# Pooled attention feeding a complex token mixer: batch 1's keys pooled by TensorE, another buffer for v's last keys, and a new order of pieces

## The chip, the cores and the metric

The kernel runs on one core of one Trainium2 chip. The metric is device time in microseconds (us) of one execution; lower is better. Before the change three runs gave 589.21, 589.93 and 592.08 us, so the median is 589.93.

## What is computed

The reference has two parts for 8 batches, 8 heads, 576 tokens and head size 64 (model width 512):

```python
k_p = k.reshape(B, H, 72, 8, D).mean(axis=3)          # 8 tokens pooled into one
v_p = v.reshape(B, H, 72, 8, D).mean(axis=3)
attn = softmax(q @ k_p^T / sqrt(D))                    # 576 x 72 per head
x = concat_heads(attn @ v_p)                           # 576 x 512 per batch
theta = x @ w_theta
y = w_tok_r @ (x * cos(theta)) + w_tok_i @ (x * sin(theta))    # mixes tokens
u = x + y
out = u + relu(u @ w_ch)
```

The weights arrive as 64-bit floats and are converted on the chip. The large products are made from high and low halves (three products each), which keeps float32 accuracy.

## The kernel before

All work is cut into named pieces. Each piece is a Python generator, and every `yield` ends one step of it. The string SCHEDULE (lines 30 to 139) names 2131 steps, and a loop at the end of the kernel runs them in that order; a letter v, g or a at the end of a name puts that step's free operation on VectorE, GpSimd (POOL) or ScalarE. So the string fixes the order on every engine and on SyncE's queue, which issues all the loads. Each engine works through its instructions in that order, and a step that waits holds back those behind it on its engine.

Names are a letter, the batch and the part:

- `k`, `v`: load pieces 0, 1 and 2 of a batch's keys or values (line 530 on). Pieces 0 and 1 hold 256 pools each, piece 2 the remaining 64; for v, piece 2 (the last keys) is stored twice, once for each half of the partitions.
- `K`, `V`: pool a piece (line 562 on). Batch 0's are pooled on TensorE, as eight matmuls with an identity that add up in PSUM (`pool_on_pe`, line 589). All later batches are pooled by adds on VectorE or GpSimd (`pool_sum`, lines 510 to 526). `K0`, `K1`, ... turn the pooled keys (`keys`, line 606), `V0`, ... scale and mask the values (`vals`, line 670).
- `Q`: load and turn q. `S`: scores and softmax of a row block of tokens. `X`: attention output x (line 871).
- `h0` to `h3`: convert w_theta. `w0.0` to `w4.0`: load and convert the token weights, real and imaginary; `W0` to `W4`: turn them on TensorE and split them into halves. `c0` to `c3`: convert w_ch.
- `T`: theta matmuls (three groups of four, line 947), sine and cosine, and the products with x. `Z`: halves of these. `M`: the token mix (line 1053, three groups of nine matmuls for one of 8 parts of a batch). `F`: the final product with w_ch (line 1081) and the output.

The order runs through an opening that loads and converts weights, does batch 0's attention and its theta, and ends with the first mix piece, `M0.0.0`. From there the pieces of neighbouring batches are interleaved. Batches 2 to 7 are handled in pairs: block 4 of the theta work holds the last 64 rows of two batches.

Buffers are shared by tags, and a tag with one buffer serves one tile at a time. The staging tile of piece 2 has the tag `kvr`, for keys and values of all batches and for one piece of batch 1's q; pieces 0 and 1 have the tag `kv`, except that batch 0's k0.1, v0.0 and v0.1 lie in parts of the still unused tile z. The low halves of x (tag `xl`, two buffers) are first written by T0.

```python
        if j < 2:
            st = staged(b, name, j, 2 * POOL * D, "kv").rearrange("p (c x) -> p c x", c=2)
        ...
        else:
            st = work([P, POOL * D], F32, "kvr", f"{name}rst{b}")
```

Of the kernel before, what the change touches and what calls it, by code (L numbers as in the profile page):

```python
# [138 lines left out]
"""

EARLY, V_ON_PE, K_ON_PE, Q_ON_PE, SUMS_ON_ACT = 2, 1, 1, 2, 2


@with_exitstack
def tile_attn_moe(
    ctx: ExitStack,
    tc: tile.TileContext,  # L150
# [1071 lines left out]
```

## Time and profile before

| | before |
|---|---|
| median of 3 runs (lowest, highest) | 589.93 us (589.21, 592.08) |
| the profiled execution | 588.76 us |
| its span, first to last instruction | 587.0 us |
| TensorE matmuls busy | 559.7 us (95%) |
| TensorE weight loads busy | 502.4 us (86%) |
| VectorE, ScalarE, GpSimd busy | 423.4, 307.5, 302.0 us |
| moved by DMA | 70.63 MB, mean 120 GB/s |
| mean granted TensorE clock | 0.984 of full speed |

The profiled execution is 588.76 us long, of which the span covers 587.0; the rest lies before the first and after the last instruction. Busy shares are shares of the span. Matmuls are pipelined and their ends are modelled, so a TensorE that is busy throughout is not at its peak. The granted clock tells how much of full speed the throttle allowed. Times within the span count from its start.

### The profile page before, as it was taken

The numbers are of one execution on the slowest core, as the hardware profiler recorded it, in microseconds if no ns is written. First come the engines' busy times: TensorE is split into PE (matmuls) and PEld (weight loads), VectorE is DVE, ScalarE is ACT, GpSimd is POOL, SyncE is SP. The second block draws the span as 40 slices with busy tenths as digits, with TensorE's granted clock in tenths as the row PEclk, the third lists the DMA queues.
The fourth block names the chain that finished last, engine by engine and source line by source line (L and its number), as shares of the span: only waits on it lengthen the run. The fifth ranks groups of instructions, "written<-read, shape, count | busy, mean of one in ns | idle before, by whom it ended". The sixth has DMA issues, their size and how long they took to land.

```text
span 587.0 us, 13259 instructions
## 1 busy us (share of the span) xinstructions
PE 559.7 (95%) x4904; PEld 502.4 (86%) x4904; DVE 423.4 (72%) x834; ACT 307.5 (52%) x628; POOL 302.0 (51%) x446
## 2 busy tenths in 40 slices
...
GB/s 276 273 261 114 121 51 79 114 129 131 80 140 133 151 130 132 120 180 127 108 131 139 152 121 119 132 182 103 94 92 145 116 80 49 55 88 9 41 26 89
DMA packets 191265, 70.63 MB, mean 120 GB/s; under 512 B 149600, under 2 KB 176224, under 8 KB 191200
## 3 DMA queue, kind: packets, MB, share of 16 engines
...
## 4 chain that ended last, share of the span: by engine, by line
PE 72%; DMA 10%; SPq 6%; DVE 5%; ACT 2%; POOL 1%; issue 1%; DVEq 0%; ACTq 0%; POOLq 0%
PE py L1053 36%; PE pt L947 14%; PE pf L1081 11%; SPq L863 2%; PE s L732 2%; DMA z<-in_v_dram 2%; SPq L1097 2%; DMA out_dram<-R 1%; DMA xt<-hall 1%; DMA wraw<-in_moe_w_tok_r_dram 1%; PE pv_av L894 1%; DMA kpst<-in_k_dram 1%; PE pv_av L885 1%; DMA qsst<-in_q_dram 1%; SPq L634 1%
## 5 line engine op out<-in xcount | busy, mean ns | idle before, releaser
L1053 PE MATMUL py<-WTh,zh 128*128 128x256 f32 (+1 forms) x576 | 87.6, 299 | 3.3 <-ACT zh L206 1.3
L1053 PE MATMUL py<-WTl,zh 128*128 128x256 f32 (+1 forms) x576 | 88.4, 298 | 0.0
L1053 PE MATMUL py<-WTh,zl 128*128 128x320 f32 (+1 forms) x576 | 86.8, 297 | 0.0
L1053 PEld LDWEIGHTS py<-WTh,zh 128*128 128x128 f32 x576 | 80.5, 190 | 7.1 <-issue 2.1
L191 POOL TENSOR_TENSOR en<-e_eps,ri 128x256 f32<-128x256 f32 (+3 forms) x74 | 44.3, 616 | 78.6 <-DVE ri L801 48.6
L1053 PEld LDWEIGHTS py<-WTh,zl 128*128 128x128 f32 x576 | 79.6, 189 | 3.0 <-issue 1.3
L1053 PEld LDWEIGHTS py<-WTl,zh 128*128 128x128 f32 x576 | 81.5, 192 | 0.7 <-issue 0.4
L191 POOL TENSOR_TENSOR zl<-z,zh 128x384 fp32r<-128x384 f32 (+1 forms) x68 | 53.4, 817 | 14.1 <-ACT zh L206 9.4
L206 ACT CAST zh<-z 128x1152 fp32r<-128x1152 f32 x22 | 25.3, 1154 | 49.1 <-PE py L1053 41.6
L947 PE MATMUL pt<-th,xh 128*128 128x512 f32 x148 | 42.4, 409 | 3.5 <-ACT xh L206 1.9
L1081 PE MATMUL pf<-uh,chh 128*128 128x256 f32 (+1 forms) x256 | 44.0, 297 | 0.0
L1081 PE MATMUL pf<-uh,chl 128*128 128x256 f32 (+1 forms) x256 | 43.6, 295 | 0.0
L1081 PE MATMUL pf<-ul,chh 128*128 128x256 f32 (+1 forms) x256 | 43.3, 295 | 0.0
L797 ACT ACTIVATE e_eps<-e_eps 128x576 f32<-128x576 f32 (+1 forms) x30 | 20.3, 678 | 43.9 <-DVE e_eps L792 43.9
L947 PE MATMUL pt<-tl,xh 128*128 128x512 f32 x148 | 40.6, 397 | 0.0
L947 PE MATMUL pt<-th,xl 128*128 128x512 f32 x148 | 40.2, 394 | 0.0
L951 ACT ACTIVATE g<-pt,c_magic 128x512 f32<-128x512 f32 x35 | 24.0, 686 | 30.5 <-PE pt L947 23.6
L1081 PEld LDWEIGHTS pf<-uh,chh 128*128 128x128 f32 x256 | 37.5, 188 | 2.5 <-issue 0.5
L1081 PEld LDWEIGHTS pf<-ul,chh 128*128 128x128 f32 x256 | 37.1, 188 | 1.1 <-issue 0.5
L1081 PEld LDWEIGHTS pf<-uh,chl 128*128 128x128 f32 x256 | 37.3, 188 | 0.7
L953 DVE SCALAR_TENSOR_TENSOR g<-g,pt 128x512 f32<-128x512 f32 x35 | 23.8, 681 | 17.2 <-ACT g L951 17.0
L947 PEld LDWEIGHTS pt<-th,xh 128*128 128x128 f32 x148 | 25.9, 192 | 9.3 <-ACT xh L206 2.5
...
## 6 DMA issues: line engine op xcount, KB each, us to landing
...
```

The costliest lines, as they stand in the source:

```text
L191: nc.gpsimd.tensor_tensor(out[:, r], a[:, r], b[:, r], op)
L206: nc.scalar.copy(out, src)
L634: queue.dma_start(st[32 * i : 32 * i + 32, S * c : S * c + S].rearrange("p (x a) -> p x a", a=32), q[b, 2 * j + c + 4 * (i // 2)].rearrang ...
L732: nc.tensor.matmul(scs[hh][o : o + 64, SP * c : SP * c + SP], qT[r, c, t0 + o : t0 + o + 64], kpT[r, c, SP * hh : SP * hh + SP], start=Tru ...
L797: nc.scalar.activation(e[:n], e[:n], AF.Exp, scale=scale)
L863: queue.dma_start(Ex[32 * j : 32 * j + 32, 0:m, i], Gx[32 * i : 32 * i + 32, 0:m, j])
L947: nc.tensor.matmul(pt, l[:, c, :], r[:, c, :], start=i == 0, stop=i == 11)
L951: nc.scalar.activation(g, pt, AF.Identity, bias=c_magic)
L953: nc.vector.scalar_tensor_tensor(g, g, MAGIC, pt, ALU.subtract, ALU.subtract)
L1053: nc.tensor.matmul(py[:, :n], l[:, kk, :], r[:, kw, t], start=i == 0, stop=i == 3 * NK - 1)
L1081: nc.tensor.matmul(pv[:, :n], l[:, kk, o], uhl[r][:, kk, t], start=i == 0, stop=i == 11)
L1097: (nc.scalar if b == B - 1 and i % 2 else nc.sync if b == B - 1 else queue).dma_start(out[b, t, ch0 : ch0 + 32].rearrange("(x t) a -> t x ...
```

## The change

Three edits. First, batch 1's keys are pooled by TensorE as well: a new function adds the eight parts of a piece in a PSUM bank of its own, one bank (tag `tp`) for each piece, and a copy on ScalarE or VectorE takes the sum to SBUF. The pieces K1.0, K1.1 and K1.2 thus have two steps instead of one. Second, batch 0's v0.2 is loaded into a buffer of the tag `xl` instead of `kvr`. Third, the order of all steps from the 31st on is new, and many steps change their engine; no step besides the three pieces' is added or taken away. The conditions in `vals` are only written in another way.

In the excerpt of the order below, the first part reaches from the 31st step to the first mix piece; the three short parts are those around the first mix piece of batches 2, 3 and 4.

```diff
-K0 K0a w0.0 w0.0 S0.0 h1 h1 S0.0 Q0.1 Q0.1 h1v h2 Q0.2 Q0.1v h1 Q0.2 Q0.2v S0.0 w1.0 S0.1 h1 Q0.4 Q0.4 S0.1 S0.0 S0.1
-h1 k1.2 Q0.3 K1.2v h3 S0.1 S0.0 Q0.4v S0.0g S0.2 Q0.3 S0.2 Q0.3v h2 v0.0 S0.2 S0.0v h1 k1.1 S0.1 S0.0 w0.1 S0.2 S0.1g
-w1.0 h2v h2 h1v S0.0v h3 S0.0 S0.1g w0.0g S0.0a h1 h3a v0.2 S0.2 S0.4 S0.3 S0.1 w0.0 S0.1a S0.1 w1.1 S0.3 S0.1v S0.3
-S0.4 h3 S0.2g w0.0 S0.2g w0.1 h3 V0.0 V0.2 w0.1v S0.4 S0.3 v0.1 h3 K1.1v w0.1 V0.1 S0.3 v1.2 w0.1 w0.0 w0.1 w3.1 S0.4
-h3 V0a w2.0 h3a W0 w1.1 V1.2g S0.3v k1.0 W0a S0.2 V0 S0.4 S0.3g S0.3 S0.2v S0.2 W0 S0.3a w1.0a w1.1a S0.2a X0.0 w1.0
-w1.1 w1.0 w2.0 X0.0a S0.4g w2.1 S0.3 X0.0v w1.1 w1.0 S0.4g X0.0a S0.3a S0.4 T0.0a W0 W0a w2.1 W0 S0.4a S0.4 S0.4v
-w2.0a w1.1 w3.0 w2.1a W1 Q1.0 h3 w2.0 w2.1 W1a w2.1 w2.0 W1 T0.0g K1.0v T0.0 w4.0 Q1.1 T0.0 T0.1a T0.0 T0.1g X0.2 w3.0
-T0.0 T0.1 w2.0 w3.0a X0.2a w3.0 Q1.0 X0.2a X0.2a v1.1 Q1.0a T0.2g w2.1 W1 W1a w3.1 T0.1 w3.1a T0.0 W1 T0.2v Q1.1 w3.0
-w3.1 Q1.1a W2 T0.2 Q1.2 w3.0 T0.1 w4.0 T0.2 X0.2g T0.0 w3.1 Q1.3 K1 T0.0 w4.0v w3.1 W2a T0.0a T0.3a V1.1v T0.2 Q1.2
-T0.0 W2 T0.3g T0.4a T0.0 v1.0 T0.1 T0.0 W3 T0.4g T0.2 T0.1 T0.2 T0.2 T0.1 w4.0 T0.1 W3a T0.1a T0.2 Q1.3 V1.0g T0.1
-T0.1 c0 T0.3 T0.3 w4.0 Q1.3a T0.2a W3 T0.3 W3 W3a T0.4 T0.1 T0.3 w4.0 W3 T0.3 T0.3 c0 T0.2 W4 T0.4 T0.2 W4a T0.2 W4
-T0.3 W4a T0.3a c0g c0 T0.4 c0 c0 T0.4 Q1.4 c0g W4 T0.3 Q1.2a T0.4 W2 K1a T0.4 K1 W2a c0a c0g T0.3 T0.4 W2 K1v T0.4
-S1.0 T0.3 T0.4 Z0.1a c1 c1 Z0.0v S1.0 c1a Q1.4 S1.0 Z0.0v u1 Q1.4a M0.0.0 c1 M0.0.0 c1 c1 Z0.1v M0.0.1 c1v c1v c2
...
-T2.4 T2.3 F1.0.0 T2.3g F1.2.0 Y3.2 T2.3v T2.4 T2.4 K4.1g F1.1.0 F1.0.0 T2.4 T2.4 F1.1.0 F1.2.1 K4 S3.1 F1.1.0 Y3.2
-F1.3.0 T2.4a T2.4 K4a K4.2g T2.4 F1.0.1 F1.2.0 T2.4 Z2.1a k5.0 E3.0 F1.3.0 Y3.2 K4 Z2.0g F1.1.0 F1.1.0 F1.3.0 K5.0g
-M2.1.0 M2.1.0 Z2.1v F1.3.0 M2.1.0 E3.0 M2.1.1 M2.1.0 Q4.0 v4.1 Z2.0g T2.4 T2.4 M2.1.1 M2.0.0 M2.1.1 T3.3v M2.1.1
...
-T3.3 M2.2.0g y3.2 F2.0.0 F2.2.0 T3.0v M2.3.1v T3.3 T3.3 F2.2.0 F2.0.0 S4.2 T3.3 T3.3a T3.3 K5.1g V5.2g F2.2.0 T3.2
-S4.2 E4.0 F2.0.0 T3.2 F2.2.0 T3.3v E4.0 T3.2 F2.0.0 T3.3v S4.2 F2.1.1 F2.2.1 T3.2 T3.2 F2.1.1 F2.2.1 K5 F2.2.1 F2.1.1
-S4.2v S4.4 F2.0.0 F2.2.0 S4.3 T3.2 F2.2.1 T3.2a S4.2g F2.1.1 S4.3 v5.1 F2.3.1 F2.3.1 F2.3.1 T3.2 T3.2g T3.2g Z3.1g
-F2.3.1 S4.2 Z3.0a F2.2.1 F2.0.1 F2.0.1 F2.0.1 F2.0.1 Q5.0 F2.2.0 S4.3 F2.1.0 F2.2.1 Z3.0g S4.3 S4.3g F2.1.0 M3.0.0
...
-T4.4 T4.4 T4.4 F3.0.0 T4.3 Y5.2 T4.3a T4.3 F3.1.0 F3.2.1 T4.3g k6.1 F3.0.0 F3.3.0 F3.3.0 T4.3v F3.0.1 F3.3.0 E5.0 T4.4
-Y5.2 T4.4 T4.4 K6.1g T4.4 F3.0.0 F3.2.0 F3.3.0 Y5.2 K6 F3.2.0 T4.4a T4.4 F3.2.0 T4.4 T4.4 Y5.2 Z4.0v K6a Z4.0v F3.2.0
-F3.0.0 K6 T5.3g E5.0 M4.0.0 F3.2.0 Z4.1a M4.0.0 M4.0.0 V6.2v M4.0.0 M4.0.1 M4.0.1 F3.0.0 M4.0.1 M4.1.0 Z4.1v Q6.0
...
+K0 h1 K0a h1 w0.0 S0.0 Q0.1 S0.0 h1a w0.0 Q0.2 Q0.1 k1.2 w0.1 h1 Q0.1v w0.0v Q0.2 Q0.3 K1.2 h1 Q0.4 S0.1 Q0.2v w0.0
+v0.1 h3 Q1.0 S0.0 S0.0 S0.2 S0.1 Q0.4 h2 S0.1 K1.2v k1.1 Q0.3 S0.0 S0.2 Q0.4v Q0.3v h1 S0.1 S0.0g S0.0g h2 h1 S0.2
+S0.1 S0.2 h2v S0.0 h2 h1v h1 S0.0v S0.2 S0.1g S0.1g S0.1 h3 S0.0 S0.3 S0.3 S0.4 S0.0a S0.1v w0.1 S0.3 h3a S0.3 S0.1
+S0.1v S0.4 v0.0 h3 w0.0 w1.0 S0.2g S0.2v w0.1v w0.0 K1.1 V0.1 S0.4 S0.4 w0.1 w1.0 h3 v0.2 h3 w0.1 V0.2 w3.0 K1.1a v1.2
+S0.3 V0.0 h3 w0.1 w1.0a V0v V0 S0.4 W0 S0.3v W0a w2.0 S0.2 V1.2g S0.2v W0 S0.2 S0.2a w1.0 S0.3g S0.4g w1.1 w1.1 S0.4g
+S0.3 S0.4 k1.0 S0.3a w1.0 S0.3 w1.1a X0.0 w1.1 w1.0 X0.0v S0.3a S0.4a w1.1 X0.0v X0.0a S0.4 W0 K1.0 w2.0 W0a h3a w2.0a
+T0.0g S0.4a W0 w2.1 h3 w1.1 w2.1 w3.1 w2.1a W1 v1.1 W1a T0.1a w3.0 w2.0 T0.0v w3.0a T0.0 w2.0 w2.1 T0.0 K1.0a T0.0 W1
+T0.0 T0.1g w2.0 X0.2 w3.0 X0.2a w2.1 X0.2a T0.1 Q1.0 K1 w3.0 Q1.1 w2.1 X0.2a w3.0 W1 T0.1 w4.0 Q1.0a W1v X0.2g T0.0
+T0.0 w3.1 Q1.1 w3.1a W1 Q1.4 T0.0 Q1.1a T0.2g V1.1v w3.1 W2 T0.2v w4.0 W2a T0.0a T0.3a T0.0 T0.1 T0.1 w3.1 T0.2 T0.0
+Q1.2 v1.0 T0.2 w4.0v w3.1 W2 T0.4g T0.0 T0.2 Q1.3 T0.1 T0.1 T0.2 T0.2 W3 T0.3g T0.1 w4.0 W3a T0.2 Q1.2 Q1.3 T0.3 W3
+T0.1a T0.1 T0.1 c0 T0.1 T0.3 T0.2 W3 W3a V1.0g Q1.3a W3 w4.0 T0.2a T0.3 T0.3 T0.4g w4.0 T0.3 c0 T0.4 T0.2 c0g T0.2
+T0.2 T0.3 W4 W4a T0.3 W4 K1a W4a T0.4 c0 c0 T0.4 c0 T0.4 W4 W2 T0.3a T0.3 K1 c0g T0.4 T0.3 T0.4 T0.4 c1 W2a W2 c0a
+T0.4 K1a T0.3 c0g T0.4 Z0.0v Q1.2a S1.0 Z0.1a c1 Q1.4 S1.0 c1a M0.0.0 Z0.0v c1 c1 c1 S1.0 M0.0.0 M0.0.1 Q1.4a c1v c2
...
+T2.4v T2.3a T2.3 T2.3g Y3.2 F1.2.0 T2.4 T2.4 F1.0.1 T2.4 T2.3v S3.1 Q4.0 T2.4 F1.1.0 T2.4 Y3.2 F1.1.0 F1.1.0 K4.1g
+T2.4 F1.0.0 K4 F1.3.0 F1.2.1 T2.4 Y3.2 k5.0 F1.1.0 T2.4a K4.2g T2.4 T2.4 F1.3.0 T2.4 K5.0g Z2.1v K4a F1.3.0 T3.3a K4
+M2.1.0 E3.0 Z2.1v F1.3.0 M2.1.0 M2.1.0 M2.1.1 Z2.0a M2.1.1 M2.1.1 E3.0 T3.3v M2.1.0 T2.4 Z2.0v M2.1.1 F1.1.0 F1.2.0
...
+T3.3 T3.3 T3.0v T3.0v F2.0.0 T3.3 v5.2 K5.1g S4.3 S4.2 T3.2v F2.0.0 F2.2.0 F2.2.0 F2.2.0 T3.3 T3.3 F2.2.0 T3.2 E4.0
+M2.3.1a T3.3 T3.3a T3.2 E4.0 T3.3 S4.2 F2.2.0 S4.2 T3.2 T3.3g M2.3.1g F2.2.1 T3.3v F2.1.1 T3.2 S4.2 F2.1.1 F2.2.1
+F2.2.1 T3.2 T3.2 F2.1.1 S4.2g F2.0.0 K5 F2.2.1 F2.3.1 F2.2.0 T3.2a S4.2g F2.1.1 F2.0.1 S4.3 T3.2 F2.3.1 F2.3.1 S4.2
+T3.2g v5.1 F2.0.1 F2.0.1 F2.3.1 F2.0.0 T3.2g Z3.0a F2.0.1 F2.2.1 S4.4 F2.2.1 S4.3 M3.0.0 F2.1.0 Q5.0 u4 K5a Z3.0g
...
+T4.4g F3.1.0 F3.0.0 T4.3 F3.1.0 T4.4v k6.1 Y5.2 T4.3 T4.4 T4.3a F3.0.1 F3.1.0 S5.1 T4.3 T4.3g T4.3v T4.4 T4.4 F3.3.0
+T4.4 F3.3.0 Y5.2 T4.4 E5.0 F3.0.0 F3.3.0 F3.3.0 T4.4 F3.0.0 T4.4 T4.4a T4.4 T4.4 F3.0.0 K6.1g T4.4 F3.2.0 v6.0 Y5.2
+Z4.0v V6.0g F3.2.0 K6 V6.2g K6a F3.2.0 E5.0 K6 Z4.1a V6g M4.0.0 F3.2.0 Z4.0v M4.1.0 M4.0.0 M4.0.0 T4.4 F3.2.0 M4.1.0
...
-EARLY, V_ON_PE, K_ON_PE, Q_ON_PE, SUMS_ON_ACT = 2, 1, 1, 2, 2
+EARLY, V_ON_PE, K_ON_PE, Q_ON_PE, SUMS_ON_ACT = 2, 1, 2, 2, 2
 
 
 @with_exitstack
@@ -546,7 +546,10 @@
                         )[j, hh],
                     )
         else:
-            st = work([P, POOL * D], F32, "kvr", f"{name}rst{b}")
+            if name == "vp" and b == 0:
+                st = work([P, POOL * D], F32, "xl", f"{name}rst{b}", bufs=2)
+            else:
+                st = work([P, POOL * D], F32, "kvr", f"{name}rst{b}")
             if name == "kp":
                 st = st[0:64]
                 nc.sync.dma_start(st, pools[512:])
@@ -561,6 +564,9 @@
 
     def pool(b, name, j, pe):
         st = stages[name, b, j]
+        if pe and b:
+            yield from pool_apart(b, name, j, st)
+            return
         if pe:
             pool_on_pe(b, name, j, st)
             yield
@@ -601,6 +607,33 @@
                 n = st.shape[0]
                 nc.tensor.matmul(rem, ident[0:n, 0:n], st[:, D * r : D * r + D], **steps[r])
 
+    def pool_apart(b, name, j, st):
+        if (name, b) not in pooled:
+            pooled[name, b] = [work([P, NC, D], F32, name, f"{name}{b}", bufs=2 if name == "vp" else 1), None]
+            if name == "kp":
+                pooled["kq", b] = pooled[name, b]
+        n = st.shape[0]
+        bk = bank([P, 512], "tp" if name == "kp" else "th", f"{name}p{b}_{j}")
+        pv = bk[:n, 0 : D if j == 2 else 2 * D]
+        if j < 2:
+            pv = pv.rearrange("p (c d) -> p c d", d=D)
+        for r in range(POOL):
+            nc.tensor.matmul(
+                pv, ident[0:n, 0:n], st[..., D * r : D * r + D], start=r == 0, stop=r == POOL - 1
+            )
+        yield
+        e = pick("av")
+        if j == 2:
+            dst = pooled[name, b][1] = work([n, D], F32, name + "r", f"{name}r{b}")
+            copy(e, dst, pv)
+        elif name == "kp":
+            copy(e, pooled[name, b][0][:, 2 * j : 2 * j + 2, :], pv)
+        elif e == "a":
+            nc.scalar.mul(pooled[name, b][0][:, 2 * j : 2 * j + 2, :], pv, 1.0 / POOL)
+        else:
+            nc.vector.tensor_scalar(pooled[name, b][0][:, 2 * j : 2 * j + 2, :], pv, 1.0 / POOL, None, ALU.mult)
+        yield
+
     Vrs, qTs, parts, er32 = {}, {}, {}, {}
 
     def keys(b):
@@ -669,7 +702,7 @@
 
     def vals(b):
         vm, vr = pooled["vp", b]
-        if b < V_ON_PE:
+        if b == 0:
             Vs[b] = work([P, NC, D], F32, "vp", f"vp{b}", bufs=2)
             nc.scalar.mul(Vs[b], vm, 1.0 / POOL)
             yield
@@ -678,7 +711,7 @@
         Vr = Vrs[b] = work([P, 2, D], F32, "Vr", f"Vr{b}", bufs=2)
         for y in range(2):
             r = slice(64 * y, 64 * y + 64)
-            (nc.vector if b < V_ON_PE else ENG[pick("vg")]).tensor_tensor(
+            (nc.vector if b == 0 else ENG[pick("vg")]).tensor_tensor(
                 Vr[r],
                 vr[r].unsqueeze(1).broadcast_to([64, 2, D]),
                 mask[r, y].unsqueeze(2).broadcast_to([64, 2, D]),
```

## Rows read from the trace of the kernel before

**Rows 1.** Page, part 1: each engine's busy us (share of the span) and instructions.

```profile
PE 559.7 (95%) x4904; PEld 502.4 (86%) x4904; DVE 423.4 (72%) x834; ACT 307.5 (52%) x628; POOL 302.0 (51%) x446
```

**Rows 2.** Stretches: from:to, length; busy PE, PEld, DVE, ACT, POOL; granted clock; DMA share; GB/s.

```profile
0.00:28.00 28.00, 22.70 (x160) 18.58 (x161) 20.56 (x49) 15.85 (x68) 8.00 (x18) 1.00 1.02 278
28.00:40.00 12.00, 8.92 (x57) 8.10 (x56) 9.10 (x21) 7.86 (x40) 3.97 (x7) 0.86 0.83 209
40.00:50.00 10.00, 8.21 (x83) 6.21 (x81) 7.87 (x15) 8.85 (x17) 3.50 (x5) 0.96 0.65 222
50.00:76.00 26.00, 26.00 (x177) 21.15 (x176) 24.00 (x41) 22.39 (x39) 10.91 (x15) 0.95 0.46 109
76.00:82.40 6.40, 3.21 (x46) 2.27 (x44) 6.19 (x14) 5.50 (x13) 2.86 (x4) 0.81 0.25 86
82.40:200.00 117.60, 117.60 (x1202) 105.91 (x1203) 97.14 (x193) 77.22 (x192) 64.67 (x96) 0.98 0.57 115
200.00:400.00 200.00, 191.77 (x1703) 171.13 (x1702) 147.10 (x282) 106.64 (x169) 125.98 (x183) 0.99 0.62 136
400.00:560.00 160.00, 159.91 (x1326) 147.93 (x1326) 100.19 (x200) 63.16 (x95) 79.65 (x117) 1.00 0.37 78
560.00:587.00 27.00, 21.33 (x166) 21.12 (x164) 11.21 (x26) 0.00 (x0) 2.52 (x4) 0.97 0.40 62
```

**Rows 3.** Chain of waits, 0 to 90 us: start us, us, what.

```profile
26.41 8.98 DMA z<-in_v_dram
...
35.53 3.65 PE vpp L599 x16
...
50.43 3.93 PE pt L947 x12
...
69.49 3.56 DMA qst<-in_q_dram
...
82.38 7.75 PE py L1053 x41
```

**Rows 4.** SyncE's issues, 0 to 90 us: start us, us, queue, line, out<-in.

```profile
25.05 2.15 SPq L542 DMA_DIRECT2D z<-in_v_dram  x2
...
33.04 1.41 SPq L555 DMA_DIRECT2D vprst<-in_v_dram  x2
...
47.60 0.52 SPq L441 DMA_DIRECT2D wraw<-in_moe_w_tok_r_dram  x1
...
54.88 1.99 SPq L542 DMA_DIRECT2D vpst<-in_v_dram  x2
```

**Rows 5.** What SyncE waited for, 0 to 90 us: us in total, times, longest.

```profile
SPq L555 <- DMA vprst<-in_v_dram: 3.1, 1, 3.1
...
SPq L555 <- PE vpp L602: 2.6, 1, 2.6
```

**Rows 6.** TensorE pools two pieces of batch 0's keys (timeline).

```profile
6.03 2.05 PE L599 MATMUL kpp<-kpst,ident 128*128 128x128 f32 x16
...
12.72 1.14 PE L602 MATMUL kpp<-kprst,ident 64*64 64x64 f32 x16
```

**Rows 7.** VectorE's adds for batch 1's keys (timeline).

```profile
20.69 0.73 DVE L521 TENSOR_TENSOR kprst<-kprst 64x256 f32<-64x256 f32 x2
...
32.26 1.14 DVE L521 TENSOR_TENSOR kpst<-kpst 128x512 f32<-128x512 f32 x2
...
52.87 1.66 DVE L521 TENSOR_TENSOR kpst<-kpst 128x512 f32<-128x512 f32 x2
...
54.56 0.29 DVE L526 TENSOR_TENSOR kp<-kpst 128x128 f32<-128x128 f32 x1
```

**Rows 8.** TensorE at the first mix piece of batches 2 and 4 (timeline).

```profile
226.04 1.71 PE L1053 MATMUL py<-WTh,zh 128*128 128x256 f32 x9 [1.30 <-ACT zh L206]
...
355.51 0.63 PE L1081 MATMUL pf<-ul,chh 128*128 128x256 f32 x4
...
360.43 1.33 PE L1053 MATMUL py<-WTh,zh 128*128 128x256 f32 x9 [0.40 <-DVE zh L208]
```

168 lines of the change are left out of this document (84 added, 84 removed).

## The prediction

> **What bounds the kernel now.** I read the page's first part, then the table of stretches, then the chain of waits of the opening, then SyncE's list of issues with what it waited for, then single instructions for prices. TensorE is busy 559.7 of 587.0 us [rows 1], so the time is its work plus its idle time, 27.3 us. The table says where that idle lies [rows 2]: 5.3 us in 0 to 28, 3.1 in 28 to 40, 1.8 in 40 to 50, none in 50 to 76, 3.2 in 76 to 82.4, none from 82.4 to 200, 8.2 from 200 to 400, almost none to 560, and 5.7 in the last stretch, which ends with output. The opening, up to the first token-mix matmul at 82.4 us, thus holds 13.4 us, half of it all, and after it batches 0 and 1 run without a gap. So the question has two halves: when does the first M0 piece start, and what happens to the gaps between 200 and 400 us?
>
> The chain of the opening [rows 3] ends its DMA part with the last piece of batch 0's v to arrive: v0.1 holds the chain for 8.98 us to 35.4 us. TensorE pools it in 3.65 us, and 15 us after the landing, at 50.43, the first theta matmul starts. From there TensorE is full until 76 us. A DMA wait of 3.56 us to 73.05 (the row names q's staging tile; what goes on after it is w_ch's conversion) and VectorE work follow, and M0 starts at 82.4.
>
> Why does v0.1 land so late? SyncE issues it at 25.05 (ready by 27.2), and then issues nothing until 33.04 [rows 4]. The issue at 33.04 is v1.2, which needs the one buffer that v0.2 sits in; it waited 3.1 us for v0.2's bytes and 2.6 us for TensorE to pool them [rows 5]. All loads share that queue, so the transfer rate falls from 278 GB/s in 0 to 28 to 209 in 28 to 40 [rows 2]. In 12 us at 69 GB/s less, 0.83 MB were not moved, or 3.0 us at the earlier rate.
>
> **The change, part by part.** The sum is made against the profiled execution, 588.76 us (span 587.0); the median of the runs is 589.93, 1.17 us above, and I carry that difference over.
>
> (a) **v0.2 in another buffer.** v1.2 no longer waits for v0.2, so the stop from 27.2 to 33.04 goes, unless another takes its place. v0.2 itself waited for k1.2 to be pooled; that goes too. By the tiles' sizes, 8.8 MB were asked for up to the end of v0 before; in the new order it is 8.5 MB, v0.2 being last. At 278 GB/s that is 30.6 us; before, the same division gives 31.7 against 35.4 measured, so 3.7 us behind. The last of v0 therefore lands between 30.6 and 34.3; I take 31.5, nearer the early end, as no stop now stands ahead of it. Gain: 3.9 us, ends 1.1 and 4.8. What is late next is v1.1's load: its buffer is that of k1.0, so it stands behind K1.0's pooling, and behind it on SyncE now stand Q1.1, w4.0, Q1.4, Q1.2, v1.0, Q1.3 and c0. Before, w4.0 was issued at 47.6 and v1.1 at 54.88 [rows 4]. In the new order both come right after K1.0's matmuls, at some 45 to 48 us, so w4.0 is about where it was and v1.1 some 7 us earlier. I cost this at nothing: W4 is turned only after three of the five theta pieces, and these fill TensorE's stretch from 50 us on [rows 2]. If w4.0 came 5 us later than that cover allows, M0 would be 5 us later.
>
> (b) **Batch 1's k on TensorE.** Batch 0's pieces show the price: 2.05 us for a 256-pool piece, 1.14 us for the rest [rows 6]. Batch 1 has two of the first and one of the second: 5.24 us more TensorE work. K1.2 (1.14) stands where TensorE idles 5.3 of 28 us, K1.1 (2.05) now stands just before v0's pooling, where it idled 3.1 of 12 us; both cost nothing there, and 3.19 us if their data came later than v0's. K1.0 (2.05) stands between X0.0 and T0.0, with 1.8 us idle in 40 to 50. I take half of it as hidden: +1.0, ends 0 and 2.05. The ScalarE or VectorE copies that follow stand in 28 to 50 us beside 5.3 idle us of ScalarE, and nothing but their bank waits for them.
>
> The Trainium skill's page "Trainium Kernel Development and Optimization" (Best Practices) says that matmul busy share is the wrong gauge of room on TensorE and that the share of weight loads is a good one. In 50 to 76 the matmul row is 26.00 of 26 and the weight-load row 21.15 [rows 2]. By the page another 4.8 us would fit there, so K1.0 would be free even if it slid past T0.0, and the sum below would be 1.0 us lower.
>
> (c) **VectorE is freed** of the same pooling: 0.73 for K1.2's first adds, 1.14 + 0.29 for K1.1, 1.66 + 0.29 for K1.0 [rows 7], together 4.1 us. Six other pieces ahead of M0 move on to VectorE and four off it, at 0.2 to 0.7 us each; I set this at nothing net, within 1.5 us. VectorE was busy 24.0 of 26 us in 50 to 76 and 6.2 of 6.4 in 76 to 82.4 [rows 2], so without its relief it, not TensorE, would keep M0 where it was. With K1.0's 1.95 us out of 52 to 55 and the weight rows handled a few us sooner in 28 to 50, where it idled 5.0 of 22 us, it can follow. I add no gain for it.
>
> (d) **The half-clock stretch.** TensorE stood idle before v0.1, and then its 16 matmuls took 3.65 us, against 2.05 for the same 16 of batch 0's k [rows 3, 6]; the granted clock of 28 to 40 is 0.86 [rows 2], so part of it ran at 1.2 instead of 2.4 GHz. With K1.1 and the other pieces of v in that hole the idle time shrinks; I take half of the 1.6 us back: -0.8, ends -1.6 and 0.
>
> (e) **The new order after M0.** Every batch has the same pieces between its milestones, shifted by about eight places, and some 150 change engine. From 82.4 to 200 and from 400 to 560 TensorE had no idle time to give back. From 200 to 400 it had 8.2 us. Nothing in the trace shows the new waits, so I bound them: all gaps gone, -8; doubled, +8. I take 0, since the places at the batch changes that I compared (below) are slightly worse and the copies moved off POOL slightly better.
>
> **Sum:** -3.9 + 1.0 - 0.8 = -3.7 us; 588.76 becomes 585.1, in terms of the runs 586.2. M0 should start near 78.7 us.
>
> **Rivals.** (1) *The opening does not move.* TensorE's full stretch begins when W1 has been converted and turned, as both orders put W1 ahead of T0.0; w1.1 is now asked for after 10.5 MB instead of 8.3, at 278 GB/s 38 us instead of 30. If that conversion, or K1.0's full 2.05 us, sets T0.0, the gain of (a) is lost: with T0.0 at 50.4 again, M0 is at 82.4 and the time 590. For it: TensorE already idled 1.8 us in 40 to 50, after v0 was pooled, so more than v0 was missing there. Against: VectorE and ScalarE, which convert W1, idled 5 us each in 28 to 50, and w0.1 now comes first.
>
> (2) *Slower: thinner cover at the batch changes.* Between the last theta matmul of a pair and its first mix matmul stand F pieces of the batch before, up to 0.63 us each [rows 8]; the work they hide is ScalarE's and VectorE's sine chain. The new order has 6 at M2 where there were 7, 12 for 14 at M3, 7 for 8 at M4. Today M2 waits 1.30 us and then takes 1.71 us for its first nine matmuls; M4 waits 0.40 and takes 1.33 [rows 8]. If each of the three loses two pieces' worth (1.3 us) and falls into a half-clock stretch that costs as much as the opening's (1.6), that is 3 x 2.9 = 8.7 us, less the opening's 3.7: 595. It decides from 3.7 us on, somewhat over one such loss. For it: M2's row shows wait and slow start together. Against: M4 waited 0.40 without a slow start, and one piece fewer is 0.63, not 1.3.
>
> (3) *Much better.* The wait in 76 to 82.4, where the granted clock is 0.81 [rows 2], shrinks as well, or half of the 8.2 us goes: 586.2 less 4 to 5, 582. Against: the order of W4, c0 and T0.4 ahead of M0 is almost unchanged.
>
> **How the numbers follow.** Forecast 586.2: 0.45. Rival 1: 0.25. Rival 2: 0.15. Rival 3: 0.15. A measurement of this kernel can tell about 0.5% (2.95 us) from no change, so faster means below 587.0, slower above 592.9. The forecast's own case reaches from 583.5 (a, b and d at their best: -6.4) to 590.9 (at their worst: +1.0), with 0.6 of it below 587.0: 0.27; rival 3 gives 0.15, the early side of rival 1 0.05: faster 0.47. Rival 2 puts 0.11 above 592.9, rival 1 with some of (e)'s loss 0.05: slower 0.16. The rest, 0.37, is the same. Range: from 580 (beyond rival 3's time) to 593; outside are rival 2's upper part and the far end of rival 3, under 2 in 10 together.
>
> **What would show it.** Right: SyncE without the stop at 27 to 33; a rate near 278 GB/s to about 40 us; the last of v0 landed by 33; T0.0's first matmul near 47; M0 near 78.7. Each failing names its step. If M0 comes near there and the time does not fall, (e) is wrong, and the table of 200 to 400 shows it; if T0.0 stays at 50 with v0 early, rival 1. The forecast is wrong if SyncE finds another stop of several us before 40 us, for instance at k1.0 or v1.1.

## The result, and the profile after

The changed kernel takes 583.39 us (median of 4 runs, 581.3 to 584.59) where the kernel before takes 590.42 in the same set (4 runs, 589.21 to 592.08): ratio 0.9897, 95% interval 0.9865 to 0.9929. A later set of both gave 583.46 (12 runs) against 588.0 (32 runs), ratio 0.992, 0.9887 to 0.9952. By the medians it is 4.5 to 7.0 us faster; the forecast was 3.7. Medians are over all runs, while the ratios leave out the few slow ones (two of run 2's ten below, one of the 32), which lie over 1.5% above their kernel's fastest. The size is about right. The place is not: the opening, where the forecast put its gain, did not move.

The profile's first part answers [rows 1]: TensorE is busy 0.9 us less, with 48 more matmuls, and idle 5.4 us less (580.7 - 558.8 = 21.9, before 27.3). ScalarE and POOL are relieved, VectorE is not.

```profile
PE 558.8 (96%) x4952; PEld 502.3 (87%) x4952; DVE 423.4 (73%) x834; ACT 297.6 (51%) x617; POOL 295.8 (51%) x445
```

The same stretches as [rows 2], with the same columns:

```profile
0.00:28.00 28.00, 23.44 (x169) 19.19 (x171) 20.62 (x48) 16.19 (x68) 6.02 (x17) 1.00 1.03 259
28.00:40.00 12.00, 9.70 (x82) 9.46 (x81) 7.01 (x16) 8.23 (x41) 1.05 (x2) 0.86 1.04 268
40.00:50.00 10.00, 8.52 (x87) 6.49 (x87) 7.84 (x16) 6.66 (x15) 4.62 (x8) 1.00 0.47 179
50.00:76.00 26.00, 26.00 (x191) 21.34 (x189) 23.90 (x41) 23.31 (x40) 11.90 (x16) 1.00 0.55 120
76.00:82.40 6.40, 3.80 (x46) 2.72 (x45) 6.18 (x13) 5.87 (x14) 2.84 (x4) 0.76 0.27 83
82.40:200.00 117.60, 117.60 (x1208) 105.77 (x1208) 95.15 (x193) 78.53 (x197) 65.67 (x100) 0.98 0.56 117
200.00:400.00 200.00, 195.05 (x1735) 174.30 (x1733) 150.95 (x287) 104.05 (x162) 126.49 (x191) 1.00 0.64 140
```

Two things are to be seen. In 28 to 40 us the transfer rate is 268 GB/s where it was 209, as forecast, and TensorE works 0.8 us more. Yet M0 starts at 82.11 us, where it started at 82.38. And from 200 to 400 us TensorE idles 4.95 us where it idled 8.2, at full granted clock.

Why did the faster loads not help? First SyncE's issues, which answer to [rows 4], with one wait that answers to [rows 5] (us in total, times, longest):

```profile
25.33 1.73 SPq L558 DMA_DIRECT2D vprst<-in_v_dram  x2
...
28.17 3.42 SPq L558 DMA_DIRECT2D vprst<-in_v_dram  x2
...
50.05 1.31 SPq L542 DMA_DIRECT2D vpst<-in_v_dram  x2
...
52.65 0.50 SPq L441 DMA_DIRECT2D wraw<-in_moe_w_tok_r_dram  x1
```

```profile
SPq L542 <- PE kpp L621: 5.7, 1, 5.7
```

The long stop from 27.2 to 33.04 is gone. Shorter ones are left: v1.2's two issues, 0.61 us each, start at 28.17 and 30.98, and in a second execution of the same kernel (run 9) SyncE waits 3.2 us, until 33.35, for VectorE to be done with a weight's buffer. And the last piece of v0 (v0.2, at 25.33) is issued no earlier than the last one was before (v0.1, at 25.05 [rows 4]).

Nor did the old stop leave the DMA engines idle. In the kernel before, with the columns of [rows 2]:

```profile
27.00:32.00 5.00, 4.45 (x38) 4.21 (x38) 4.65 (x12) 4.70 (x20) 3.03 (x4) 1.00 1.04 196
32.00:36.00 4.00, 1.48 (x13) 1.37 (x12) 3.93 (x9) 3.78 (x24) 0.00 (x0) 0.95 0.50 127
```

Through five of the stop's six us their share was 1.04, as high as before it; what they moved fell to 196 GB/s all the same. Only from 32 us on, with no load issued after v0.1 until 33.04, did the share fall. Why v0.1 needs 9 us is not shown. Then TensorE and POOL in the opening:

```profile
31.09 3.35 PE L621 MATMUL kpp<-kpst,ident 128*128 128x128 f32 x16 [2.30 <-DVE en L844]
34.23 2.30 PE L605 MATMUL vpp<-z,ident 128*128 128x128 f32 x16
36.37 1.90 PE L608 MATMUL vpp<-vprst,ident 128*128 128x64 f32 x16
38.10 2.00 PE L605 MATMUL vpp<-z,ident 128*128 128x128 f32 x16
```

```profile
40.41 1.84 POOL L191 TENSOR_TENSOR vprst<-vprst 128x256 f32<-128x256 f32 x2 [11.36 <-DMA vprst<-in_v_dram]
...
43.40 1.56 POOL L191 TENSOR_TENSOR en<-e_eps,ri 64x256 f32<-64x256 f32 x3 [0.38 <-PE per L869]
```

TensorE stands 2.30 us before K1.1 (the profile names a step of VectorE that had just ended) and then pools it at half clock (3.35 us; the same product took 2.05 in [rows 6]). V0's three products are queued behind it and end at 40.1 us; before they ended at 39.2. This wait is one execution's: in run 9, the same kernel, K1.1 starts without one and takes 1.95 us, and TensorE stands 1.98 us for v0.2 instead. POOL stands 11.36 us for v1.2, with S0.4's sums behind, which then wait 0.38 us more for TensorE. v1.2, though issued earlier, is not there earlier; its adds in the kernel before:

```profile
37.46 1.25 POOL L191 TENSOR_TENSOR vprst<-vprst 128x256 f32<-128x256 f32 x2 [7.35 <-DMA chl_st<-in_moe_w_tok_i_dram]
```

X0.0 starts at 45.28 (before 42.76) and T0.0 at 51.40 (before 50.23).

The first mix products, which answer to [rows 8], and batch 3's first theta product, which in the kernel before waited 0.80 us:

```profile
225.01 1.29 PE L1086 MATMUL py<-WTh,zh 128*128 128x256 f32 x9 [0.64 <-DVE zh L208]
...
354.98 2.31 PE L1086 MATMUL py<-WTh,zh 128*128 128x256 f32 x18 [0.33 <-DVE zh L208]
```

```profile
247.20 1.09 PE L980 MATMUL pt<-th,xh 128*128 128x512 f32 x4
```

M2 is reached 1.0 us earlier than before, M4 5.5 us earlier, and TensorE's last product ends 6.6 us earlier. In these two executions most of the gain lies behind M2.

### The profile page after: what moved, and what is told of

Its sections match the earlier page's. It is cut to its first block, busy times and chain, and to the rows that moved or that the text cites. A ratio compares the mean times of both kernels' runs of the same rounds, so it can differ in the third digit from the quotient of the medians.

```text
span 580.7 us, 13326 instructions
## 1 busy us (share of the span) xinstructions
PE 558.8 (96%) x4952; PEld 502.3 (87%) x4952; DVE 423.4 (73%) x834; ACT 297.6 (51%) x617; POOL 295.8 (51%) x445
## 4 chain that ended last, share of the span: by engine, by line
PE 83%; SPq 4%; DVE 4%; POOL 2%; DMA 2%; ACT 2%; issue 1%; DVEq 0%; POOLq 0%; ACTq 0%
PE py L1086 38%; PE pt L980 16%; PE pf L1114 14%; PE s L765 2%; SPq L896 2%; SPq L1130 1%; PE pv_av L918 1%; PE pv_av L927 1%; DMA out_dram<-R 1%; PE pv_px L918 1%; PE s_av L765 1%; PE wt L461 1%; PE kpp L621 1%; DMA qst<-in_q_dram 1%; PE ths L416 1%
## 5 line engine op out<-in xcount | busy, mean ns | idle before, releaser
L191 POOL TENSOR_TENSOR en<-e_eps,ri 128x256 f32<-128x256 f32 (+3 forms) x77 | 42.5, 574 | 67.5 <-DVE ri L834 58.1
L191 POOL TENSOR_TENSOR zl<-z,zh 128x384 fp32r<-128x384 f32 (+1 forms) x64 | 49.5, 804 | 17.8 <-ACT zh L206 11.5
L984 ACT ACTIVATE g<-pt,c_magic 128x512 f32<-128x512 f32 x35 | 24.0, 687 | 44.8 <-PE pt L980 40.1
L1092 DVE TENSOR_TENSOR xb<-py,xb 128x320 f32<-128x320 f32 x32 | 15.3, 479 | 24.0 <-PE py L1086 24.0
```

The costliest lines, as they stand in the source:

```text
L191: nc.gpsimd.tensor_tensor(out[:, r], a[:, r], b[:, r], op)
L984: nc.scalar.activation(g, pt, AF.Identity, bias=c_magic)
L1092: nc.vector.tensor_tensor(u, py[:, :n], u, ALU.add)
```

## The experiments

Theory: the new order after M0 made the gain, and the edits of the opening gave nothing. Rival: the opening's edits (earlier loads, VectorE freed) are felt later on. All kernels keep the computation whole.

The table has one profiled execution of each. M0, M2 and M4 are the starts of each batch's first mix product; up to each mark both orders have done the same products of T, M and F. Times in us.

```
kernel                          median (runs)  ratio [95%]              M0     M0-M2   M2-M4   M4-end
before                          -              -                        82.38  143.66  134.39  220.90
after                           583.39 (4)     0.9897 [0.9865, 0.9929]  82.11  142.90  129.97  219.71
1  new order alone              583.43 (4)     0.9892 [0.9845, 0.9938]  80.94  143.62  132.22  220.09
2  opening alone                586.24 (10)    0.9955 [0.9919, 0.9992]  81.08  144.43  132.47  220.07
3  new order from M2 on         583.86 (4)     0.9898 [0.9850, 0.9945]  79.39  142.88  133.01  219.87
4  after, V1.2 and K1.1 behind  586.32 (10)    0.9954 [0.9920, 0.9988]  85.16  144.36  128.68  219.43
5  one stretch new              593.88 (6)     1.0097 [1.0074, 1.0120]  80.39  143.53  141.48  219.95
6  new letters, old order       591.61 (6)     1.0083 [1.0053, 1.0113]  79.52  144.65  136.98  222.57
7  buffer alone                 589.34 (12)    1.0019 [0.9997, 1.0040]  82.37  143.33  133.71  220.07
8  K1 on TensorE alone          587.23 (12)    0.9993 [0.9973, 1.0014]  84.14  147.55  131.29  220.06
9  after, again                 583.46 (12)    0.9920 [0.9887, 0.9952]  81.39  143.63  128.54  220.54
10 opening alone, again         586.88 (12)    0.9993 [0.9962, 1.0024]  83.30  144.86  134.56  220.07
11 new order, old letters       594.47 (9)     1.0099 [1.0064, 1.0134]  81.17  149.79  133.43  219.80
12 after, V1.2 alone behind     582.48 (12)    0.9915 [0.9879, 0.9951]  81.01  143.62  129.99  220.01
```

Runs 1 to 4, 5 to 8 and 9 to 12 each had the kernel before beside them: 589.02, 588.16 and 588.0 us.

**Which half? Runs 1, 2, 3, 9, 10.** Run 1 is the kernel before up to M0.0.0, then the words of after, without the steps that its opening has already done:

```diff
 c1a Q1.4 S1.0 Z0.0v u1 Q1.4a
-M0.0.0 c1 M0.0.0 c1 c1 Z0.1v M0.0.1 c1v c1v c2 M0.0.1 M0.0.1 S1.0 S1.1
+M0.0.0 c1 c1 c1 M0.0.0 M0.0.1 c1v c2 M0.0.0 M0.0.1 Z0.1v c1v S1.0 M0.0.1
...
```

> The kernel before with its own opening (all steps up to M0.0.0's first, without the buffer and without batch 1's k on TensorE), and from there the order and the engine letters of the kernel after. Theory (the gain lies behind M0 and is the new order's own): M0.0.0 stays at 82.4 us as before, T3.1 comes near 247.5 us instead of 250.84, T4.0 near 296.8 instead of 303.14, and the time is 583.5 to 584.5 us, 6 us under the kernel before. Rival (the opening's edits reach on: earlier loads, or the 4.1 us of VectorE set free by K1): 588.5 to 590.5 us, T4.0 near 302 us.

It takes 583.43 us: the whole gain, without the buffer and without K1 on TensorE. T4.0 came at 296.18. Run 2 is the reverse, after's code and opening with before's words behind it; four steps that before has done by then come first:

```diff
 S1.0 c1a
-M0.0.0 Z0.0v c1 c1 c1 S1.0 M0.0.0 M0.0.1 Q1.4a c1v c2
+S1.0 Z0.0v u1 Q1.4a M0.0.0 c1 M0.0.0 c1 c1 Z0.1v M0.0.1 c1v c1v c2 M0.0.1
...
```

> The kernel after with its opening whole (buffer for v0.2, batch 1's k on TensorE, its order up to M0.0.0's first), and from there the order and the letters of the kernel before. Theory: M0.0.0 near 82.1 us, T4.0 near 303 us, and the time is 589.5 to 590.5 us, no more than 0.5 us from the kernel before. Rival (the opening's edits reach on): 583.5 to 586 us with T4.0 near 297 us. A third case, both are needed: this one and the order alone each give about half, 586 to 588 us.

It took 586.24 us, the number of the third case, and its interval is clear of 1. So it was run again beside after itself:

> The kernel with after's opening and before's order behind it once more, with more rounds: the first time it came out 2.8 us under the kernel before (ratio 0.9955), while the buffer alone and batch 1's k on TensorE alone changed nothing. Theory (the opening gives nothing, or little): 0 to 1.5 us under the kernel before, M0.0.0 at 80 to 83 us. Rival (the opening as a whole, with its own order, gives a part of the gain): 2 to 3.5 us under the kernel before, and M0.0.0 under 80.5 us or less half clock behind it.

> The kernel after, unchanged, as the yardstick of this set, and a second profiled execution of it. The three profiled executions of the opening of before had M0.0.0 at 79.4, 80.9 and 82.4 us, the two of after's opening at 81.1 and 82.1, so one execution's opening says little. Theory: M0.0.0 between 80.5 and 83 us again, M0.0.0 to the end of TensorE's work near 492.6 us as in the first profile (before: 498.95), and the time 5 to 7 us under the kernel before. Rival (the first profile was a lucky one behind M0, since the new order alone took 495.93 us there): 495 to 496 us for that part and 4 us under the kernel before.

Now the opening alone is 0.9993, with no change well inside the interval; after keeps its gain, and M0 to the end took 492.71 us in it, as in its first profile (492.58). What both intervals of the opening alone allow is 0.9962 to 0.9992, so a gain of 0.5 to 2.2 us is not ruled out. The traces show none: before's opening reaches T0.0 at 47.31 to 50.23 us and M0 at 79.39 to 82.38 in six executions (before, 1, 3, 5, 6, 11), after's at 50.35 to 52.54 and 81.08 to 83.30 in four (after, 2, 9, 10). M0 is 1.3 us later in the mean. Run 3 takes the new words from M2.1.0 on only:

```diff
 Z2.0g F1.1.0 F1.1.0 F1.3.0 K5.0g
-M2.1.0 M2.1.0 Z2.1v F1.3.0 M2.1.0 E3.0 M2.1.1 M2.1.0 Q4.0 v4.1 Z2.0g T2.4
+T3.3a M2.1.0 Z2.1v F1.3.0 M2.1.0 M2.1.0 M2.1.1 M2.1.1 M2.1.1 E3.0 T3.3v M2.1.0 T2.4 Z2.0v
...
```

> The kernel before with its own order up to batch 2's first mix product (M2.1.0), and the order and letters of after from there. Theory: what was gained between M2.1.0 (226.04 us in the kernel before, 1.0 us later than after) and T4.0 (303.14, 6.6 later) is made behind M2.1.0, so M2.1.0 stays at 226.0 us, T4.0 comes near 297.5 us and the time is 584 to 585.5 us. Rival (the zh copies and xh copies ahead of M2, at 200 to 226 us, are what counts): T4.0 near 300 us and 587 to 588 us. If the gain hangs on the whole order since M0: 589 to 590 us.

It takes 583.86 us, so by its runs most of the gain is made behind M2. Its one profiled execution does not place it so: M2 to M4 took 133.01 us, as with the old order, and M0 to the end 495.76. T4.0 as a mark, which these expectations use, flatters the new order: before has M3.1.1's third group of nine products ahead of T4.0, after has it behind, some 1.3 us of work. M4 has no such shift, hence the table's columns.

Averaged over the five executions with before's order behind M0 (before, 2, 7, 8, 10) and the five with after's (after, 1, 4, 9, 12), the parts are 144.8 against 143.6, 133.3 against 129.9 and 220.2 against 220.0: 4.8 us, of which 3.4 lie between M2 and M4. As a whole this gain is clear: M0 to the end takes 497.0 to 499.5 us in the five with the old order, 492.5 to 495.9 in the five with the new. Its split is less so. From M2 to M4 the two ranges overlap (131.29 in run 8, 132.22 in run 1), and the 1.2 us from M0 to M2 rest mostly on run 8: runs 3 and 5, with the old order up to M2, took 142.88 and 143.53. The stretch from 200 to 300 us shows in what form (columns as above; before and run 10, then after and run 9):

```profile
200.00:300.00 100.00, 95.62 (x810) 86.16 (x809) 72.04 (x140) 52.45 (x87) 66.30 (x96) 0.98 0.61 131
```

```profile
200.00:300.00 100.00, 94.76 (x844) 84.69 (x836) 71.69 (x136) 53.91 (x89) 64.78 (x95) 0.97 0.61 130
```

```profile
200.00:300.00 100.00, 97.08 (x858) 87.40 (x857) 75.88 (x148) 51.67 (x81) 65.17 (x101) 1.00 0.65 139
```

```profile
200.00:300.00 100.00, 96.55 (x853) 86.92 (x852) 75.59 (x146) 51.06 (x81) 63.55 (x100) 1.00 0.66 139
```

In the mean of the five, TensorE idles 4.7 us there with the old order and 3.2 with the new; in 300 to 400 us 3.1 and 2.3. The clock granted in 200 to 300 averages 0.98 and 0.996; 0.016 of 100 us, an estimate, is another 1.6 us. That is 3.9 of the 4.8; the rest lies inside time that the profile calls busy.

One gap of it can be followed back. Before batch 3's first theta product (T3.1) TensorE waits in all five executions with the old order, 1.8 us in the mean, and in none of the five with the new. (Run 5 below, with the new order from M2 on and the old one ahead of it, waits 0.57 us.) The rows, one from each of before, 2, 7, 8 and 10 (the answering row of after, 247.20, stands above, without a wait):

```profile
250.84 1.20 PE L947 MATMUL pt<-th,xh 128*128 128x512 f32 x4 [0.80 <-ACT xh L206]
```

```profile
250.31 1.20 PE L979 MATMUL pt<-th,xh 128*128 128x512 f32 x4 [2.32 <-ACT xh L205]
```

```profile
250.55 1.23 PE L950 MATMUL pt<-th,xh 128*128 128x512 f32 x4 [2.35 <-ACT xh L206]
```

```profile
254.75 1.20 PE L976 MATMUL pt<-th,xh 128*128 128x512 f32 x4 [0.58 <-ACT xh L205]
```

```profile
253.80 2.07 PE L979 MATMUL pt<-th,xh 128*128 128x512 f32 x4 [3.06 <-ACT xh L205]
```

xh is cast from x, and x is copied out of three banks. The last copies and casts on ScalarE, and what VectorE did meanwhile, in the kernel before:

```profile
249.55 0.59 ACT L206 COPY xa<-pv_s 128x512 f32<-128x512 f32 x1 [3.41 <-DVE xs L917]
250.17 0.62 ACT L206 CAST xh<-xa 128x512 fp32r<-128x512 f32 x1
```

```profile
247.39 0.43 DVE L917 STREAM_TRANSPOSE xs<-pv_px 128x256 f32<-128x256 f32 x1
247.76 0.75 DVE L521 TENSOR_TENSOR vprst<-vprst 128x256 f32<-128x256 f32 x2
248.55 0.23 DVE L526 TENSOR_TENSOR vpr<-vprst 128x64 f32<-128x64 f32 x1
248.69 0.77 DVE L917 STREAM_TRANSPOSE xs<-pv_s 128x256 f32<-128x256 f32 x2
```

The third copy stands behind Y3.0's transposes of the same banks (pv_s), and those stand behind V4.2's adds (0.75 and 0.23 us) on VectorE. The two only read pv_s, yet not at once: the copy starts 0.09 us after the transposes end. The Trainium skill's page "PSUM — Partial Sum Buffer" (PSUM bank collisions raise a hardware error) gives a reason for keeping two engines apart on one bank, reads included; the trace agrees in that these readers run one after the other here, in the order in which the program names them. The same in the kernel after:

```profile
244.51 0.59 ACT L206 COPY xa<-pv_s 128x512 f32<-128x512 f32 x1
...
245.30 0.63 ACT L206 CAST xh<-xa 128x512 fp32r<-128x512 f32 x1
```

```profile
244.19 0.42 DVE L208 COPY xa<-pv_av 128x256 f32<-128x256 f32 x1
...
245.69 0.77 DVE L950 STREAM_TRANSPOSE xs<-pv_s 128x256 f32<-128x256 f32 x2
```

The copy now stands ahead of the transposes, VectorE takes one of the three copies, and V4.2 runs on POOL. xh starts 1.9 us ahead of T3.1's product instead of 0.7 us. It is so in all ten executions: with the old order the copy waits 3.34 to 3.82 us for the transposes, with the new it starts 1.1 to 1.2 us ahead of them. That these three moves, and not others nearby, close the gap was not tried one by one.

**The opening's parts. Runs 7, 8, 4, 12.** Run 7 changes one line of the kernel before:

```diff
-            st = work([P, POOL * D], F32, "kvr", f"{name}rst{b}")
+            if name == "vp" and b == 0:
+                st = work([P, POOL * D], F32, "xl", f"{name}rst{b}", bufs=2)
+            else:
+                st = work([P, POOL * D], F32, "kvr", f"{name}rst{b}")
```

> The kernel before with one line changed: v0.2 lands in the buffer of x's low halves; order, letters and K1 as before. Prediction's step (a) taken alone: SyncE's stop at 27.2 to 33.04 us goes, v0.2 lands 3.5 to 4 us earlier, V0's pooling ends near 36 us instead of 39.2, T0.0's first product near 47 us and M0.0.0 near 79 us, and the time is 585 to 587 us. Rival (T0.0 is set by W1, K1.0 and S0's sums; the stretch to 76 us is full): V0's pooling ends earlier, X0.0 by at most 1 us, T0.0 stays between 48 and 51 us, M0.0.0 between 79.4 and 82.4 us as in the three profiled executions of this opening, and the time is within 1 us of the kernel before.

No gain (1.0019). SyncE's v1.2 moves from 33.04 to 27.93, and v0.1, issued ahead of it, arrives as late as ever; before, TensorE started this product at 35.53 [rows 3]:

```profile
26.04 1.79 SPq L542 DMA_DIRECT2D z<-in_v_dram  x2
27.93 2.35 SPq L558 DMA_DIRECT2D vprst<-in_v_dram  x2
```

```profile
36.32 3.53 PE L602 MATMUL vpp<-z,ident 128*128 128x128 f32 x16 [2.86 <-DMA z<-in_v_dram]
```

T0.0 came at 50.63, M0 at 82.37. The stop stood behind v0.1's issue and could not make v0.1 late.

Run 8 has K1 on TensorE and nothing else:

```diff
-EARLY, V_ON_PE, K_ON_PE, Q_ON_PE, SUMS_ON_ACT = 2, 1, 1, 2, 2
+EARLY, V_ON_PE, K_ON_PE, Q_ON_PE, SUMS_ON_ACT = 2, 1, 2, 2, 2
...
-h1 k1.2 Q0.3 K1.2v h3
+h1 k1.2 Q0.3 K1.2 K1.2v h3
```

> The kernel before with batch 1's k pooled by TensorE, each product at the place where VectorE's adds stood, its copy right behind it on ScalarE (K1.1, K1.0) or VectorE (K1.2); buffers and the rest of the order as before. Prediction's step (b) taken alone: 5.24 us more work on TensorE, of which 4.2 us lie in its waits and up to 1 us does not, 4.1 us less on VectorE; M0.0.0 within 1 us of before's 79.4 to 82.4 us and the time within 1 us of the kernel before. Rival (VectorE's freed 4.1 us are worth something, since the softening's sums wait for it): M0.0.0 under 79.4 us, the time 2 to 3 us under the kernel before. Other rival (TensorE waits for k1.1 as it does in after, 2.30 us with what is queued behind it): T0.0 behind 51 us and the time 1 to 2 us over the kernel before.

0.9993: 5.24 us more on TensorE and 4.1 less on VectorE cancel: the interval reaches from 1.6 us gained to 0.8 lost. The profiled execution had a late T0.0 (53.10) and M0 (84.14); the runs as a whole do not show that as a loss.

Runs 4 and 12 try to mend after's opening by two moves:

```diff
-S0.2 V1.2g S0.2v
+S0.2 S0.2v
...
-w1.1 w1.1 S0.4g S0.3
+w1.1 w1.1 S0.4g V1.2g S0.3
...
-w0.0 K1.1 V0.1
+w0.0 V0.1
...
-w3.0 K1.1a v1.2
+w3.0 v1.2
...
-V0.0 h3 w0.1 w1.0a V0v V0 S0.4
+V0.0 K1.1 h3 w0.1 w1.0a V0v V0 K1.1a S0.4
```

> The kernel after with two steps of its opening moved: V1.2's adds behind S0.4's sums on POOL, and K1.1's product and copy behind V0.0's on TensorE. Theory of why the opening did not move (POOL stood 11.36 us for v1.2 with S0.3's and S0.4's sums behind it; TensorE stood 2.30 us for K1.1 with V0's pooling behind it): V0's pooling ends near 36 us instead of 40.1, X0.0 starts near 43 us instead of 45.28, T0.0 comes 1 to 3 us earlier than 51.40 and M0.0.0 with it, 79.5 to 81 us; the time is 581 to 582.5 us. Rival (T0.0 is set by W1 or by K1.0 and the stretch to 76 us is full of work anyway): X0.0 moves, T0.0 and M0.0.0 by less than 0.5 us, the time within 1 us of after, 583 to 584 us.

A miss: M0 came at 85.16. k1.0 loads into the buffer that K1.1 reads, so its issue slid from 35.57 to 42.90 us, and TensorE, rid of K1.1, stood 3.14 us for v0.2 instead:

```profile
42.90 0.38 SPq L538 DMA_DIRECT2D kpst<-in_k_dram  x1
```

```profile
35.65 2.49 PE L607 MATMUL vpp<-vprst,ident 128*128 128x64 f32 x16 [3.14 <-DMA vprst<-in_v_dram]
```

Run 12 has only V1.2's move (the first two pairs of lines):

> The kernel after with V1.2's adds behind S0.4's sums on POOL and nothing else moved; with K1.1 moved as well, k1.0's load came 7 us later (42.90 instead of 35.57 us), since it waits for K1.1's buffer, and the opening became longer. Theory (POOL's 2 us for V1.2 stand ahead of S0.4's sums, for which X0.0 waits): X0.0 starts 1 to 2 us earlier than the 44 to 45 us of after's opening, T0.0 near 49 us, M0.0.0 near 80.5 us, 0.5 to 1.5 us under after. Rival (W1's turn and K1.0 set T0.0): T0.0 stays at 50.4 to 51.4 us and the time within 1 us of after.

X0.0 starts at 43.9 (44.55 in run 9), T0.0 at 50.28 (50.67): about the rival's case. At 582.48 against 583.46 us it is the lowest median of all, but the two intervals are almost one, so it can't be called better than after.

**Inside the order. Runs 5, 6, 11.** Run 6 keeps before's order and takes after's engines from M0 on, 137 letters; run 11 takes the order and keeps the letters:

```diff
-F1.0.1 F1.2.0 T2.4 Z2.1a k5.0 E3.0
+F1.0.1 F1.2.0 T2.4 Z2.1v k5.0 E3.0
...
```

> The order of the kernel before throughout; from M0.0.0's first on, each step runs on the engine that after names for it (137 of its letters change, among them Z2's casts from ScalarE and POOL to VectorE and T3.1's and T3.3's). Theory (the gaps of before stood behind casts on ScalarE that came late, so the letters carry most): M2.1.0 to T4.0 in 73 to 74 us instead of 77.10, 585.5 to 587 us in all. Rival (the place of the steps in each engine's queue carries it): the stretch stays at 76 to 78 us and the time at 588.5 to 590 us, or longer, since letters chosen for another order load an engine at the wrong moment.

> The kernel before, its opening kept; from M0.0.0's first step the order of after, but each step on the engine that before names for it. The counterpart of the letters alone, which cost 3.4 us. Theory (order and letters were found together; the stretch from M2.1.0 to T4.0 needs both): the stretch at 73 to 76 us instead of 71.5, and 587 to 591 us in all. Rival (the order is what counts, the letters are decoration): the stretch near 71.5 to 72.5 us and 583.5 to 585 us in all.

Each alone makes the kernel slower, by 0.8% and 1.0%; together they make it 0.8 to 1.1% faster. Neither is decoration. Where they lose was followed only so far: run 11 takes 149.79 us from M0 to M2, with its longest wait (2.16 us) just ahead of M2, and the longest of run 6's new waits is for a cast on ScalarE, at M3's first product:

```profile
287.30 1.33 PE L1052 MATMUL py<-WTh,zh 128*128 128x256 f32 x9 [2.21 <-ACT zh L205]
```

Run 5 takes after's words between M2.1.0 and T4.0 only; its first seam is run 3's.

> The kernel before, its opening and its order, but for one stretch: the 272 steps from M2.1.0's first to T4.0's first product stand in the order and with the letters of after (what is left of that stretch follows in the order of before). In the profiled executions so far this stretch took 77.10 us (before) and 77.19 (the opening alone), 71.51 (after), 71.63 (the new order alone) and 73.47 where only the steps behind M2.1.0 were new. Theory (the gain of the new order is made in this stretch): 71.5 to 73.5 us for the stretch, 584.5 to 586 us in all, 3.5 to 5 under the kernel before. Rival (the stretch shifts work into the next: what is gained by T4.0 is given back by M4.0.0): the stretch as short, but T4.0 to M4.0.0 over 60 us instead of 57.29, and 588 to 589 us in all.

593.88 us, slower than both cases, and M2 to M4 took 141.48. T4.0 came 74.66 us after M2, and M4 66.82 after T4.0, over the rival's 60, but for a reason that neither had: a wait at the second seam.

```profile
304.87 5.07 SPq L862 DMA_DIRECT2D eraw<-G  x8
310.03 2.05 SPq L1096 DMA_DIRECT2D out_dram<-R  x4
```

```profile
313.53 0.51 DVE L1091 STREAM_TRANSPOSE R<-xb 128x320 f32<-128x320 f32 x1 [14.01 <-DMA out_dram<-R]
```

```profile
314.56 2.74 PE L1052 MATMUL py<-WTh,zl 128*128 128x320 f32 x9 [9.89 <-DVE xb L1058]
```

An output's DMA had slid behind E4.2's eight issues on SyncE; VectorE stood 14.01 us for the buffer, and TensorE 9.89 us for VectorE. Without these 9.89 us M2 to M4 would be 131.6 us, an estimate, near the new order's 129.9. As a test of what the stretch is worth alone the run failed; it shows what one misplaced transpose and its output cost.

## Why the prediction was right and wrong

**(a) failed**, at the step "The last of v0 therefore lands between 30.6 and 34.3; I take 31.5". In after's opening TensorE's wait for it ended at 35.56 (run 9), 35.25 (run 2), 35.79 (run 10) and 34.92 (run 12); before it landed at 35.4, and in six executions of that opening TensorE's wait for it ended between 34.24 and 36.41. The forecast divided all bytes by a rate, as if one queue's stop delayed everything ("All loads share that queue, so the transfer rate falls"); but the DMA engines were busy through most of the stop, at a share of 1.04. And [rows 3, 4] held the answer: v0.1 was issued at 25.05, 2 us before the stop began, and its own transfer held the chain for 8.98 us. The new last piece is issued at 25.33 and takes about as long: in run 2 from 25.53 to 35.25. The rate did rise to 268 GB/s, but neither v0.2 nor v1.2 landed earlier for it. Of the loads behind, w4.0 was put "about where it was" and came at 52.65 us instead of 47.60; no cost of that shows, as TensorE stayed full to 76 us. Run 7 has the step by itself: -0.2 to +2.4 us, instead of -3.9.

**(b)** K1 on TensorE was put at +1.0 net of cover, ends 0 and 2.05; run 8, which has VectorE's relief in it too, shows -1.6 to +0.8 us. The size holds roughly. K1.1, costed at nothing, is where TensorE waited 2.30 us in the first profile, but not in run 9. Whether K1.0 was free, as the Trainium skill's page "Trainium Kernel Development and Optimization" (Best Practices) would have it by the weight-load share, or cost something that VectorE's relief gave back, that interval cannot tell.

**(c)** VectorE's freed time, counted as nothing, is in the same interval. **(d)** The half-clock stretch of the opening is not a matter of this change, so its -0.8 did not come: the granted clock of 28 to 40 us is 0.86 in both first profiles, and 1.00 in run 3 with the old opening as in run 2 with the new.

**(e) was mis-sized:** taken as 0 within 8 us, it measured -4.8 in the traces, about all of the gain. The step that failed is "the places at the batch changes that I compared ... are slightly worse": the F pieces that cover a wait were counted, not what stands ahead of the last copy and cast on ScalarE and VectorE. That this is what counted is shown at T3.1 alone. The places that the forecast compared did not decide: M2 has one covering piece fewer, and in the first profiles it waits 0.64 us instead of 1.30 [rows 8], as zh's first cast is now VectorE's (0.76 us) and no longer ScalarE's (1.15); but over the five executions of each order M2 waits 0.64 us in the mean with the new and 0.67 with the old (0.28 to 1.30), and M4 0.30 and 0.21.

**The rivals.** Rival 1 was right about the opening: T0.0 at 51.40, M0 at 82.11, and the opening alone gains 2.2 us at most in what both of its intervals allow. K1.0's product (2.00 us) and a weight's turn do run up to T0.0 without a gap in the first profile, as it said; that they set it was not tried. Rival 2 failed: M2 and M4 wait about as long as before. Rival 3, at 0.15, named the place ("half of the 8.2 us goes"; 3.3 of them went in the first profile), though its other half, the wait in 76 to 82.4, stayed: 2.6 us idle there instead of 3.2. Its 582 us counted this on top of the opening's gain, so it too came near by luck. The forecast's number came near by luck: a wrong term of -3.9 stood where the right one of -4.8 was set to 0.
